# A new written-out order for a delta-rule attention with routed attention experts, and two GpSimd scalings in four pieces

## The chip, the cores and the metric

The kernel runs on one core of a Trainium2 chip. The metric is the device time of one execution in microseconds. Shown are three runs of the kernel before, and one profiled execution, from which all rows come. PE is TensorE, DVE is VectorE, ACT is ScalarE, POOL is GpSimd, SP is SyncE, which here only issues DMAs.

## The reference

The first half is linear attention with a delta rule, for 4 batches, 8 heads, 768 tokens and a head size of 48:

```python
k_n = k / (np.linalg.norm(k, axis=-1, keepdims=True) + 1e-06)
for t in range(S):
    y[:, :, t] = np.einsum('bhd,bhde->bhe', q[:, :, t], state)
    v_old = np.einsum('bhde,bhd->bhe', state, kt)
    state = state + bt[..., None] * np.einsum('bhd,bhe->bhde', kt, vt - v_old)
```

The second half takes y as x (768 tokens by 384 for each batch) and runs 4 attention experts of head size 64 over it, causal, with softmax; each token's two best experts by `x @ w_gate` are weighted by a softmax over the two and summed after the output projection `wo`.

## The kernel before

**Units and chunks.** The tokens are worked as 6 units `n` (0 to 5): units 0 to 2 are the three stretches of 256 tokens of the first pair of batches, 3 to 5 those of the second. A unit has 4 chunks `c` of 64 tokens, and a chunk has 16 heads (2 batches by 8 heads). Within a chunk the delta rule is a triangular system, so each unit needs the inverse of 32x32 triangular blocks, all 128 partitions by 32x32 at a time, and then a correction between the halves of each 64-token block.

**The inverse of a unit.** `gk` (TensorE) makes the Gram products of the keys, `ek` copies them to TN and TG. `si` transposes on VectorE into BB. `pre.n.0` to `pre.n.7` are small instructions on 32 columns: inverse square roots of the diagonal by Newton steps (`rr`, `g`, `nn`), then the scales `aa` and `na`; the last number of the token says VectorE (1) or GpSimd (2). `pa` multiplies BB (128 x 32 x 32) by `aa`, `sv.n.1` to `sv.n.30` are elimination steps (each a product into `tp` and a subtraction from `bl`, of i x (31 - i) columns), `sv.n.31` a triangular mask, `pz` a second scaling and a copy of the diagonal. Then `so` and `sn` transpose back, `sc1` copies halves, `ma` and `mb` (TensorE) join the halves, and `ea` and `eb` (8 small copies each from PSUM) follow them. Unit 0 has another way: `en` masks the Gram blocks, `sb.1` to `sb.15` eliminate 16x16 blocks on VectorE, and `zx`, `zp`, `ze` finish each chunk's inverse by block products on TensorE.

**The recurrence.** For each chunk: `gq` and `eq` make the masked query-key products `pm`, `vt` scales the values (kv by `nt`), `ks` multiplies the keys with the state SB, `ex` subtracts this from the values into XB, `uu` applies the inverse, `eu` copies, `st` and `es` update the state, `yq` and `yu` make the output, `eh` and `el` split it into a rounded part and a rest in XH, and `hx` moves rows between partitions by DMA.

**The experts.** Per unit and batch: `pj`, `ph`, `pl` are queries and keys, `pv`, `ev`, `eg` values and gate logits, `gates` the routing, `mx`, `em`, `mp`, `mr`, `er` the row maxima ahead of the softmax, `sc`, `xp`, `av`, `oa` scores, exponentials, weighted values and their copy, `nm`, `on` the normalization, `ft`, `fh`, `fl`, `fo`, `eo`, `do` the projection and the store.

**What sets the order.** Tiles are scheduled by hand: the string `ORDER` lists about 1390 tokens, each the name of a small function with its arguments, `name.args:bank`. A loop at the end of the kernel calls them one by one, and every engine issues its own instructions in that order, so the list is at once the program of five in-order queues. For functions with an engine argument, 0 is ScalarE, 1 VectorE and 2 GpSimd. The digit behind the colon is one of four PSUM buffers `ps0` to `ps3` of two banks each. `fill.n` issues n matmuls of zeros, which nothing reads. `lk`, `lh`, `lv`, `lw`, `lc` are loads on SyncE's queue (`lh` with a last 1 on ScalarE's); weights are loaded into the tiles AT, rounded by `wh` on ScalarE, and `wl` takes the rest. `eq.n.c.0` is a copy on ScalarE and a masking product on GpSimd, `eq.n.c.1` one product on VectorE straight from PSUM.

The line numbers that the rows name: L182 all matmuls, L186 and L188 copies on ScalarE and VectorE, L302 `wl`, L351 `en`, L358 `eq`, L362 `si`, L382 to L404 `pre`, L408 `pa`, L412 `pz`, L422 and L424 `sv`, L427 `zt`, L438 and L439 `sb`, L454 `sn`, L458 `so`, L473 `zx`, L531 `vt`, L540 `ex`, L704 the end of `mp`, L763 to L765 `nm`, L768 `on`.

Of the kernel before, what the change touches and what calls it, by code (L numbers as in the profile page):

```python
# [47 lines left out]
gq.0.1:1 eq.0.1.0:1 gq.0.0:2 sn.0 zx.0.0.0 zx.1.0.0 fill.15:0 zp.0.0:0 lw.6 zp.0.1:0 wh.1.0 si.1 pre.1.0.1 zx.0.1.0  # L48
wl.4.2 vt.0.2.2 wh.6.1 ze.0.1.0:0 zp.1.0:3 ze.0.0.0:0 pre.1.1.2 zx.1.1.0 zp.1.1:3 ze.1.1.1:3 wl.6.1 lk.2.0 pre.1.2.1
pre.1.3.2 zp.0.2:1 wl.1.2 wh.5.0 zp.0.3:1 ze.1.0.0:3 ze.0.3.0:1 ze.0.2.0:1 zp.1.2:0 zp.1.3:0 pre.1.4.1 pre.1.5.2  # L50
zp.0.4:3 eq.0.0.1:2 ze.1.3.0:0 ze.1.2.0:0 ze.0.4.0:3 vt.0.0.2 fill.4:1 uu.0.0:1 zx.2.0.0 eu.0.0.0:1 pa.1.1 pre.1.6.1
sv.1.1.1 sv.1.2.1 zp.1.4:2 zx.3.0.0 st.0.0:3 zp.2.0:0 ze.2.0.0:0 es.0.0:3 yu.0.0:1 fill.2:3 zp.2.1:0 sv.1.3.2 sv.1.4.2
sv.1.5.1 yq.0.1:3 eh.0.0.0:1 zx.2.1.0 ze.1.4.0:2 ze.2.1.0:0 pre.1.7.2 el.0.0:1 sv.1.6.1 sv.1.7.1 ks.0.1:1 zx.3.1.0
zp.2.2:2 ex.0.1:1 uu.0.1:0 zp.3.0:1 ze.2.2.0:2 fill.2:0 zp.2.3:2 sv.1.8.2 sv.1.9.2 ze.2.3.0:2 sv.1.10.2 sv.1.11.2
sv.1.12.1 wl.5.2 sv.1.13.2 eu.0.1.0:0 ze.3.0.0:1 yu.0.1:3 st.0.1:0 es.0.1:0 eh.0.1.1:3 zp.3.1:1 fill.5:2 zp.2.4:2
ze.2.4.0:2 el.0.1:3 lv.1.0 lv.0.3 ze.3.1.1:1 ks.0.2:0 gq.0.3:3 ex.0.2:0 lk.2.1 eq.0.3.1:3 yq.0.2:1 sv.1.14.2 sv.1.15.2
sv.1.16.1 fill.7:2 uu.0.2:2 sv.1.17.1 zp.3.2:0 sv.1.18.1 zp.3.3:0 sv.1.19.1 eu.0.2.0:2 yu.0.2:1 fill.5:3 st.0.2:3
ze.3.2.0:0 ze.3.3.0:0 lk.2.2 vt.0.3.2 vt.1.0.2 hx.0.0 es.0.2:3 zp.3.4:2 eh.0.2.1:1 sv.1.20.2 el.0.2:1 sv.1.21.2
sv.1.22.2 ks.0.3:0 sv.1.23.1 ex.0.3:0 yq.0.3:3 ze.3.4.0:2 uu.0.3:2 lv.1.1 vt.1.1.1 eu.0.3.0:2 vo gk.2.1:1 fill.2:0
yu.0.3:3 eh.0.3.1:3 sv.1.24.2 ek.2.1.0:1 sv.1.25.2 sv.1.26.2 gq.1.0:0 el.0.3:3 eq.1.0.1:0 sv.1.27.2 sv.1.28.2  # L60
sv.1.29.2 fill.8:2 st.0.3:2 sv.1.30.2 sv.1.31.2 gk.2.2:1 gk.2.0:3 ek.2.2.0:1 es.0.3:2 lk.2.3 pv.0.0:0 hx.0.1 lv.1.2
ek.2.0.1:3 ev.0.0.1:0 gk.2.3:2 ks.1.0:1 gq.1.2:3 eg.0.0:0 pj.0.0.0:0 pz.1.2 ek.2.3.0:2 eq.1.2.0:3 so.1 si.2 pre.2.0.1
sc1.1.1.0 sc1.1.0.0 pre.2.1.2 ph.0.0.0.0:0 ex.1.0:1 pl.0.0.0:0 pre.2.2.1 pj.0.0.1:2 ma.1:3 sn.1 vt.1.2.2 pre.2.3.2
pre.2.4.1 ea.1.0.1.0.1:3 gq.1.1:1 eq.1.1.0:1 pre.2.5.2 ea.1.0.1.1.1:3 pa.2.2 sv.2.1.2 sv.2.2.2 sv.2.3.2 ea.1.1.1.0.1:3
ea.1.1.0.0.0:3 pre.2.6.1 sv.2.4.2 sv.2.5.2 pv.0.1:0 ea.1.0.0.1.0:3 ph.0.0.1.0:2 pj.0.1.1:1 ea.1.1.0.1.0:3
ea.1.1.1.1.0:3 ea.1.0.0.0.0:3 ph.0.1.1.0:1 mb.1:3 eg.0.1:0 gates.0.0 sv.2.6.2 sv.2.7.2 eb.1.0.1.1.0:3 pl.0.0.1:2
sv.2.8.2 sv.2.9.2 ev.0.1.1:0 pre.2.7.1 eb.1.1.0.0.0:3 eb.1.0.0.1.0:3 eb.1.0.1.0.0:3 eb.1.1.1.0.0:3 pj.0.1.0:2
ph.0.1.0.0:2 eb.1.1.0.1.1:3 eb.1.1.1.1.1:3 yq.1.0:0 eb.1.0.0.0.1:3 pl.0.1.1:1 uu.1.0:3 mx.0.0.0.0:1 lk.3.0 pl.0.1.0:2
mx.0.0.1.0:2 eu.1.0.0:3 em.0.0.0.0:1 yu.1.0:0 mx.0.1.1.0:3 em.0.0.1.0:2 eh.1.0.0:0 st.1.0:1 lv.1.3 gq.1.3:2 el.1.0:0
mp.0.0.2 es.1.0:1 mr.0.0:0 er.0.0.0:0 mx.0.1.0.0:1 em.0.1.1.0:3 em.0.1.0.0:1 sv.2.10.2 sc.0.0.0.0:0 eq.1.3.0:2  # L70
xp.0.0.0.0:0 ks.1.1:3 gk.3.0:2 yq.1.1:1 ek.3.0.0:2 mp.0.1.1 mr.0.1:0 er.0.1.0:0 ex.1.1:3 lk.3.1 sc.0.0.1.0:3 uu.1.1:2
# [101 lines left out]
def tile_kernel(ctx, tc, kq, kv, beta, wqk, wvg, wo, consts, out):  # L173
# [232 lines left out]
    def pa(n, e):  # L406
        BL = BB[n % 2]
        (V, G)[e - 1].tensor_tensor(BL, BL, aa[n % 2][:, None, :].to_broadcast([128, 32, 32]), op=OP.mult)  # L408

    def pz(n, e):  # L410
        BL, a = BB[n % 2], aa[n % 2]
        (V, G)[e - 1].tensor_tensor(BL, BL, na[n % 2][:, :, None].to_broadcast([128, 32, 32]), op=OP.mult)  # L412
# [470 lines left out]
```

## Time and profile before

| | |
|---|---|
| median of 3 runs | 448.09 us (445.79 to 450.54) |
| the profiled execution's own time | 449.58 us |
| its span, first to last instruction | 447.9 us |
| mean granted TensorE clock | 0.937 |
| busy: TensorE, VectorE, GpSimd, ScalarE | 391.5, 301.2, 219.8, 180.8 us |
| instructions: matmuls, VectorE, GpSimd, ScalarE | 10444, 598, 381, 344 |

In the rows below, a row of the timeline has the start and the duration in us, the engine, the line, the operation, what it writes and reads, its shape and count, and in brackets the idle time of the engine before it with what ended it. A row of the grouped view has the count, the busy time in us, the mean of one in ns and the idle time ahead of the group. PE rows of several matmuls are merged.

### The profile page before, as it was taken

What the parts mean: (1) busy time and instruction counts of PE and PEld (TensorE: products, weight loads), DVE (VectorE), ACT (ScalarE), POOL (GpSimd) and SP (SyncE); (2) the same over time, 40 slices, a digit from 0 to 9 for tenths busy, and PEclk for the clock granted to TensorE, in tenths of its full rate; (3) what the DMA queues carried; (4) which work ended last, traced back from release to release, by engine and by line L of the source; (5) the groups of instructions that cost most, each with busy time, mean ns of one, the idle gap of its engine ahead of it and who ended that gap; (6) DMA issues with size and microseconds to landing.
All of it is one profiled execution on the core that took longest, in us unless ns stands there. A gap on an engine that the chain in (4) does not pass through costs nothing.

```text
span 447.9 us, 22876 instructions
## 1 busy us (share of the span) xinstructions
PE 391.5 (87%) x10444; PEld 356.2 (80%) x10444; DVE 301.2 (67%) x598; ACT 180.8 (40%) x344; POOL 219.8 (49%) x381
## 2 busy tenths in 40 slices
...
PEclk9685998999999969999869799998999999999999
...
GB/s 195 258 154 1 5 96 103 81 14 50 99 70 95 127 1 121 82 110 50 6 33 128 77 40 58 1 37 4 91 74 84 84 21 3 23 37 37 3 4 72
DMA packets 15441, 29.45 MB, mean 66 GB/s; under 512 B 2800, under 2 KB 8944, under 8 KB 15344
## 3 DMA queue, kind: packets, MB, share of 16 engines
...
q10 hardware_dynamic: 256, 0.39, 0.4%
...
## 4 chain that ended last, share of the span: by engine, by line
PE 54%; DVE 23%; POOL 11%; issue 5%; ACT 4%; DMA 2%; ACTq 0%; DVEq 0%; POOLq 0%
PE ps L182 54%; POOL bl L422 3%; POOL tp L424 3%; DVE mx L686 2%; DVE bl L362 2%; DMA kq<-in_kq_dram 2%; POOL bl L408 2%; DVE bl L439 2%; DVE xh L592 1%; DVE tn L438 1%; DVE tt L458 1%; DVE tp L424 1%; ACT tt L186 1%; POOL kv L531 1%; DVE sb L564 1%
## 5 line engine op out<-in xcount | busy, mean ns | idle before, releaser
L424 POOL TENSOR_TENSOR tp<-bl 128x84 f32<-128x84 f32 (+13 forms) x128 | 63.6, 497 | 29.8 <-DVE bl L422 19.0
L422 POOL TENSOR_TENSOR bl<-bl,tp 128x84 f32<-128x84 f32 (+13 forms) x128 | 67.7, 529 | 10.0
L745 ACT ACTIVATE at<-ps 128x768 f32<-128x768 f32 (+1 forms) x48 | 43.1, 918 | 42.2 <-PE ps L182 40.3
L686 DVE TENSOR_REDUCE mx<-ps 128x2 f32<-128x1024 f32 (+3 forms) x48 | 44.2, 950 | 9.8 <-PE ps L182 9.7
L182 PE MATMUL ps<-xh,wqkh 128*128 128x256 f32 x288 | 44.7, 292 | 0.0
L182 PE MATMUL ps<-vs,at 128*64 128x65 f32 x1344 | 43.6, 223 | 0.0
L182 PE MATMUL ps<-kq 48*64 48x64 f32 x1536 | 34.4, 229 | 9.8 <-DMA kq<-in_kq_dram 5.7
L182 PEld LDWEIGHTS ps<-vs,at 128*64 128x64 f32 x1344 | 40.8, 138 | 2.2 <-issue 0.9
L186 ACT ACTIVATE tt<-ps 32x256 f32<-32x256 f32 (+2 forms) x83 | 32.1, 386 | 22.3 <-PE ps L182 19.4
L358 POOL TENSOR_TENSOR pm<-pm,cst 128x512 f32<-128x512 f32 x14 | 18.0, 1283 | 45.1 <-ACT pm L357 45.0
L182 PEld LDWEIGHTS ps<-kq 48*64 48x64 f32 x1536 | 29.0, 141 | 13.7 <-issue 6.4
L182 PEld LDWEIGHTS ps<-xh,wqkh 128*128 128x128 f32 x288 | 38.6, 194 | 1.3 <-ACT ot L186 0.4
L182 PE MATMUL ps<-qh,kh 64*128 64x256 f32 x192 | 34.9, 354 | 0.0
L182 PEld LDWEIGHTS <-ide 64*128 64x128 bf16 (+1 forms) x516 | 26.9, 100 | 6.8 <-issue 1.9
L182 PE MATMUL ps<-ql,kh 64*128 64x256 f32 x192 | 28.1, 283 | 0.0
L182 PE MATMUL ps<-qh,kl 64*128 64x256 f32 x192 | 27.8, 280 | 0.0
L182 PE MATMUL ps<-mr,sel 64*128 64x256 bf16 x192 | 27.3, 271 | 0.0
L182 PE MATMUL ps<-mask,ide 64*128 64x128 bf16 (+1 forms) x384 | 25.6, 208 | 1.4 <-issue 1.4
L182 PE MATMUL ps<-kh,qh 64*128 64x512 f32 (+3 forms) x128 | 24.9, 415 | 1.3 <-DVE kl L621 1.0
L182 PE MATMUL ps<-xh,wqkl 128*128 128x256 f32 x144 | 25.5, 287 | 0.0
L182 PE MATMUL ps<-wvgh,xh 128*128 128x260 f32 x144 | 25.4, 300 | 0.0
L186 ACT ACTIVATE ub<-ps 128x384 f32<-128x384 f32 x20 | 9.8, 490 | 35.6 <-PE ps L182 28.2
...
## 6 DMA issues: line engine op xcount, KB each, us to landing
...
```

Source lines behind the costliest of these rows:

```text
L182: T.matmul(o, lhsT=a, rhs=b, start=start, stop=stop, skip_group_check=True)
L186: S.activation(o, x, AF.Copy, **({} if scale is None else {"scale": scale}))
L358: (V if e else G).tensor_tensor(t, P if e else t, pmask[:, None, None, :].to_broadcast([128, 2, 4, 64]), op=OP.mult)
L362: V.transpose(BB[n % 2], d.rearrange("p t j -> p j t"))
L408: (V, G)[e - 1].tensor_tensor(BL, BL, aa[n % 2][:, None, :].to_broadcast([128, 32, 32]), op=OP.mult)
L422: e.tensor_tensor(X[:, a:b, i + 1:], X[:, a:b, i + 1:], tv, op=OP.subtract)
L424: e.tensor_tensor(tv, R[:, :, i + 1:].to_broadcast([128, w, m]), X[:, a:b, i:i + 1].to_broadcast([128, w, m]), op=OP.mult)
L438: E.tensor_tensor(tv, BD[:, :, i:i + 1, i + 1:].to_broadcast([128, 2, i, m]), BD[:, :, 0:i, i:i + 1].to_broadcast([128, 2, i, m]), op=OP.mult)
L439: E.tensor_tensor(x, x, tv, op=OP.add)
L458: V.transpose(d.rearrange("p t i -> p i t"), BB[n % 2].rearrange("p l i -> p i l"))
L686: V.tensor_reduce(d, two(k)[:, :, a:a + 128 * (k1 - k0)], axis=AX.X, op=OP.max)
L745: S.activation(at_of(n, b, y, kp)[:, :, 0:w], two(k)[:, :, 0:w], AF.Exp, scale=0.125)
```

## The change

`ORDER` is replaced as a whole: nearly the same tokens (1387 for 1395) in another order, with other PSUM buffers and, for part of them, other engines. By the list, the tokens that change their engine are, in numbers (before, after):

| token | engine | before | after |
|---|---|---|---|
| eq | VectorE alone / ScalarE and GpSimd | 10 / 14 | 17 / 7 |
| oa | VectorE / ScalarE | 12 / 12 | 3 / 21 |
| ea | VectorE / ScalarE | 17 / 23 | 14 / 26 |
| eb | VectorE / ScalarE | 15 / 25 | 11 / 29 |
| eh | VectorE / ScalarE | 8 / 16 | 5 / 19 |
| ph | VectorE / ScalarE | 5 / 19 | 7 / 17 |
| ev | VectorE / ScalarE | 4 / 8 | 2 / 10 |
| mp | VectorE / GpSimd | 6 / 6 | 3 / 9 |
| sv | VectorE / GpSimd | 22 / 133 | 27 / 128 |
| pa | VectorE / GpSimd | 1 / 4 | 0 / 5 |
| pz | VectorE / GpSimd | 1 / 4 | 1 / 4 |
| vt | VectorE / GpSimd | 7 / 17 | 6 / 18 |
| fill | matmuls | 132 in 18 places | 126 in 10 places |

One or two tokens each of `en`, `zx`, `ek`, `ze`, `eu`, `er`, `on`, `fh`, `sc1` and `wh` change too. The second part of the change: where `pa` or `pz` runs on GpSimd (e = 2), it is four instructions of 8 x 32 columns in place of one of 32 x 32; on VectorE (e = 1) it stays one.

The start and the end of the list, and a stretch around the join of unit 2, after the change:

```diff
+lz lc.0 zg init lh.0.2.0.0 lh.0.3.0.1 fill.22:0 gk.0.2:0 lh.0.1.0.1 lh.0.0.0.0 lc.1 lw.5 en.2.1:0 ed.2:0 gk.0.3:1
+gk.0.1:2 gk.0.0:3 ed.3:1 ed.1:2 ed.0:3 lw.3 en.3.0:1 si.0 pre.0.0.1 lw.0 pre.0.1.1 lh.0.3.1.0 pre.0.2.1 en.1.0:2
+wh.3.0 wh.5.0 pre.0.3.1 lh.0.2.1.0 pre.0.4.1 pre.0.6.1 pre.0.5.1 lk.1.3 wh.0.0 wl.0.2 lk.1.0 fill.36:0 gk.1.0:0
+gk.1.3:1 zt pre.0.7.1 sb.1.1 sb.2.1 lc.2 lk.1.2 lk.1.1 lh.0.0.1.0 en.0.0:3 sb.3.1 sb.4.1 sb.5.1 sb.6.1 sb.7.1 sb.8.1
+sb.9.1 sb.10.1 sb.11.1 sb.12.1 sb.13.1 sb.14.1 sb.15.1 fill.17:2 gq.0.0:2 lv.0.2 ek.1.0.0:0 cb wl.3.2 zm ek.1.3.0:1
+gk.1.1:3 lw.4 so.0 gk.1.2:0 sn.0 ek.1.1.0:3 lw.6 wh.6.0 ek.1.2.0:0 wh.4.0 lv.0.0 gq.0.2:1 vt.0.0.2 lw.1 lh.0.1.1.0
+wl.4.2 eq.0.0.0:2 zx.0.0.0 gq.0.1:3 lv.0.1 si.1 pre.1.0.1 eq.0.1.0:3 zx.1.0.0 pre.1.1.1 zx.0.1.0 fill.6:0 zp.0.0:0
...
+pre.3.1.2 eq.2.2.0:2 fo.0.1.1:1 pre.3.2.1 ma.2:3 eo.0.1.0:1 sn.2 ea.2.0.0.0.1:3 do.0.1 pre.3.3.2 ks.2.0:0
+ea.2.0.1.1.0:3 vt.2.2.2 ea.2.1.1.1.0:3 ea.2.1.1.0.0:3 ea.2.0.0.1.0:3 ea.2.1.0.0.0:3 pre.3.4.1 ea.2.0.1.0.0:3
+ea.2.1.0.1.0:3 ex.2.0:0 pre.3.5.2 pv.1.1:1 pj.1.1.1:2 ph.1.1.1.0:2 ev.1.1.0:1 eg.1.1:1 pre.3.7.2 mx.1.0.1.0:0
+gates.1.1 mx.1.0.0.0:1 em.1.0.1.0:0 mb.2:3 pl.1.1.1:2 em.1.0.0.0:1 pj.1.1.0:0 yq.2.0:2 eb.2.1.1.1.0:3 eb.2.0.0.1.0:3
...
+fo.5.0.1:0 eo.5.0.0:0 do.5.0 av.5.1.1.2:2 oa.5.1.1.0:2 nm.5.1 on.5.1.1 fill.18:1 ft.5.1:1 fh.5.1.0:1 fl.5.1:1
+fill.14:3 fo.5.1.0:3 fo.5.1.1:3 eo.5.1.0:3 do.5.1
...
     def pa(n, e):
-        BL = BB[n % 2]
-        (V, G)[e - 1].tensor_tensor(BL, BL, aa[n % 2][:, None, :].to_broadcast([128, 32, 32]), op=OP.mult)
+        for q in range(e * e):
+            BL = BB[n % 2][:, 32 // (e * e) * q:32 // (e * e) * (q + 1)]
+            (V, G)[e - 1].tensor_tensor(BL, BL, aa[n % 2][:, None, :].to_broadcast([128, 32 // (e * e), 32]), op=OP.mult)
 
     def pz(n, e):
         BL, a = BB[n % 2], aa[n % 2]
-        (V, G)[e - 1].tensor_tensor(BL, BL, na[n % 2][:, :, None].to_broadcast([128, 32, 32]), op=OP.mult)
+        for q in range(e * e):
+            w = slice(32 // (e * e) * q, 32 // (e * e) * (q + 1))
+            (V, G)[e - 1].tensor_tensor(BL[:, w], BL[:, w], na[n % 2][:, w, None].to_broadcast([128, 32 // (e * e), 32]), op=OP.mult)
         (V, G)[e - 1].tensor_copy(BL.rearrange("p j i -> p (j i)")[:, 0:1024:33], a)
```

The same stretches of the list before:

```diff
-lz lc.0 lh.0.3.0.1 fill.22:0 gk.0.3:0 lh.0.1.0.1 lh.0.2.0.0 ed.3:0 fill.1:1 gk.0.1:1 ed.1:1 gk.0.2:2 ed.2:2 lh.0.0.0.0
-gk.0.0:3 ed.0:3 si.0 init lk.1.2 pre.0.0.1 pre.0.1.1 pre.0.2.1 lc.2 lh.0.3.1.0 pre.0.3.1 pre.0.4.1 lw.2 en.1.0:1
-en.2.0:2 zm lh.0.0.1.0 lh.0.2.1.0 pre.0.6.1 lk.1.0 lc.1 pre.0.5.1 en.3.0:0 zt pre.0.7.1 gk.1.2:1 ek.1.2.0:1 cb sb.1.1
-sb.2.1 sb.3.1 gk.1.0:2 lw.0 wh.2.0 lw.3 gq.0.2:1 sb.4.1 sb.5.1 en.0.0:3 eq.0.2.0:1 sb.6.1 lv.0.1 sb.7.1 lh.0.1.1.0
-lk.1.1 sb.8.1 zg wh.3.0 lk.1.3 fill.28:0 gk.1.1:0 wh.0.0 sb.9.1 sb.10.1 sb.11.1 sb.12.1 sb.13.1 sb.14.1 sb.15.1 wl.0.2
-wl.2.2 lw.4 lv.0.2 lw.5 wl.3.2 so.0 fill.5:3 gk.1.3:3 lw.1 lv.0.0 ek.1.0.0:2 ek.1.1.0:0 vt.0.1.2 wh.4.0 ek.1.3.0:3
...
-ea.2.1.1.0.0:0 lk.4.0 pre.3.3.2 ea.2.0.0.0.0:0 pre.3.4.1 ea.2.1.1.1.1:0
-pre.3.5.2 pre.3.7.1 ea.2.0.0.1.1:0 ea.2.0.1.0.0:0 ea.2.0.1.1.1:0 eg.1.1:2 do.0.1 gates.1.1 vt.2.2.2
-ea.2.1.0.0.0:0 ea.2.1.0.1.0:0 ev.1.1.0:2 ph.1.1.1.0:3 mb.2:0 eb.2.0.1.0.0:0 eb.2.0.0.1.0:0 eb.2.1.0.0.1:0
...
-do.5.0 on.5.1.1 fill.8:0 ft.5.1:0 fh.5.1.0:0 fl.5.1:0 fill.8:1 fo.5.1.0:1 fo.5.1.1:1 eo.5.1.0:1 do.5.1
```

More of the change, by code (lines that the diff above doesn't have):

```diff
@@ L47 @@
-wl.2.2 lw.4 lv.0.2 lw.5 wl.3.2 so.0 fill.5:3 gk.1.3:3 lw.1 lv.0.0 ek.1.0.0:2 ek.1.1.0:0 vt.0.1.2 wh.4.0 ek.1.3.0:3
[L48 to L71, printed above, removed]
```

209 lines of the change are left out of this document (114 added, 95 removed).

## The prediction

> **What bounds the kernel now.** I read the page first: span, engines, granted clock, chain. Then the busy time by stage, the first 50 us engine by engine, the waits of TensorE, and the grouped rows of what the change touches. From the page:
>
> ```profile
> span 447.9 us, 22876 instructions
> ...
> PE 391.5 (87%) x10444; PEld 356.2 (80%) x10444; DVE 301.2 (67%) x598; ACT 180.8 (40%) x344; POOL 219.8 (49%) x381
> ...
> PEclk9685998999999969999869799998999999999999
> ...
> PE 54%; DVE 23%; POOL 11%; issue 5%; ACT 4%; DMA 2%; ACTq 0%; DVEq 0%; POOLq 0%
> ```
>
> TensorE is busy for 87% and has 54% of the chain; the other half of the chain is VectorE and GpSimd, so what can be won is where TensorE waits. The stages (columns: stretch, its length, busy time and instructions of PE, PEld, DVE, ACT, POOL, granted clock, DMA share, GB/s):
>
> ```profile
> 0.00:37.75 37.75, 18.40 (x424) 15.90 (x424) 28.66 (x57) 15.66 (x38) 17.97 (x22) 0.76 0.69 180
> 37.75:349.70 311.95, 281.22 (x8001) 257.12 (x8002) 221.79 (x432) 131.88 (x258) 196.92 (x352) 0.94 0.22 63
> 349.70:443.60 93.90, 91.90 (x2020) 83.16 (x2020) 50.79 (x111) 32.48 (x48) 4.87 (x7) 1.00 0.10 28
> 159.60:166.40 6.80, 6.57 (x102) 6.26 (x106) 3.62 (x10) 3.09 (x8) 5.86 (x13) 0.50 0.01 2
> 214.20:217.60 3.40, 3.40 (x16) 3.40 (x17) 2.63 (x3) 0.00 (x0) 2.77 (x9) 0.50 0.00 0
> 224.40:231.20 6.80, 6.64 (x112) 5.58 (x116) 3.76 (x11) 2.42 (x7) 6.04 (x10) 0.50 0.00 0
> ```
>
> The start, up to the first product of the block inverse at 37.75, leaves TensorE idle for 37.75 - 18.40 = 19.4 us. The middle, up to the first state product of the last unit at 349.70, leaves it idle for 311.95 - 281.22 = 30.7 us, and in places at half clock: the last three rows are three such stretches, 6.8, 3.4 and 6.8 us at 0.50. The end is full (91.90 of 93.90) at full clock: there a new order can win next to nothing.
>
> **The start, part by part.** The path is VectorE's: transpose, inverse square root, 15 elimination steps of unit 0, transpose, then one ScalarE copy, then TensorE. VectorE first, then GpSimd, then TensorE:
>
> ```profile
> 11.91 0.92 DVE L382 TENSOR_SCALAR g<-bl 128x32 int32<-128x32 int32 x1
> ...
> 24.98 1.24 DVE L439 TENSOR_TENSOR bl<-bl,tn 128x100 f32<-128x100 f32 x1
> ...
> 29.08 0.78 DVE L439 TENSOR_TENSOR bl<-bl,tn 128x112 f32<-128x112 f32 x1
> ...
> 31.41 0.26 DVE L439 TENSOR_TENSOR bl<-bl,tn 128x100 f32<-128x100 f32 x1
> ...
> 33.79 0.69 DVE L441 TENSOR_TENSOR bl<-bl,aa 128x512 f32<-128x512 f32 x1
> 34.75 1.91 DVE L458 STREAM_TRANSPOSE vs<-bl 128x1024 f32<-128x1024 f32 x1
> ```
>
> ```profile
> 24.79 1.31 POOL L302 TENSOR_TENSOR wvgl<-at,wvgh 128x512 fp32r<-128x512 f32 x1
> ...
> 28.88 0.85 POOL L531 TENSOR_TENSOR kv<-kv,nt 128x384 f32<-128x384 f32 x1
> ```
>
> ```profile
> 37.75 1.97 PE L182 MATMUL ps<-tt,vs 64*64 64x64 f32 x32 [11.32 <-ACT vs L473]
> ```
>
> The same product of 100 columns takes 1.24 us while GpSimd works (24.79 to 26.10) and 0.26 us once GpSimd has stopped (its last one ends at 29.73). From 11.91 (0.92 us) to 29.08 (0.78 us) there are 12 such drawn-out VectorE instructions, 13.0 us in all; eleven of them at about 0.2 to 0.27 and one of 512 columns at 0.69 would be 3.1. So some 9.9 us of this path are VectorE standing behind 12 GpSimd instructions, about 0.8 us for each.
>
> In the new order GpSimd has fewer of them in that stretch. One of the three masks of the units' diagonal blocks that it made goes to VectorE (en.2); the pm product of chunk 2 goes to VectorE and those of chunks 0 and 1 move behind the elimination in the queue; wl.2 moves behind it; the memset zg goes to the front. Left beside the path are en.1's end, wl.0, zt, en.0 and wl.3, five; two or three more (vt.0.0, wl.4, the pm product of chunk 0) come as soon as their loads land, perhaps after the path has ended. Five to eight at 0.8 us are 4.0 to 6.4 us, so the path wins 9.9 less that: 3.5 to 5.9. I take 5.
>
> Against it stand two moves. ScalarE now runs `init` (a table load and a small activation) ahead of its two loads lh.0.3 and lh.0.1, so these leave later; the path needs all four chunks, of which two are SyncE's, and the queue is no shorter than before: 0 to 1.5 us, I take 0.5. And en.2 (0.69 us, by the 512-column row) stands on VectorE ahead of three of the four `ed`, which wait for their loads anyway: nothing, 0.7 if the loads are early. lw.4 and the loads behind it on SyncE now wait for `cb`, and the last that TensorE needs ahead of the inverse, lh.0.1.1, has 5.4 MB ahead of or in it: at the 180 KB per us of the first row it lands at about 30 us, when the first product would come at 33 anyway; a lower rate costs what it is late by, 1 to 2 us. The start: -4.5, bounds -6 and +1.
>
> **The middle.** VectorE, then GpSimd, then TensorE, at three of its places:
>
> ```profile
> 155.28 2.37 DVE L404 TENSOR_SCALAR na<-aa 128x32 f32<-128x32 f32 x1
> ...
> 209.35 0.20 DVE L764 RECIPROCAL rsm<-rsm 128x8 f32<-128x8 f32 x1
> 209.59 1.99 DVE L765 TENSOR_TENSOR rsm<-gt,rsm 128x8 f32<-128x8 f32 x1
> ...
> 212.22 0.17 DVE L404 TENSOR_SCALAR na<-aa 128x32 f32<-128x32 f32 x1
> ```
>
> ```profile
> 155.25 2.36 POOL L408 TENSOR_TENSOR bl<-bl,aa 128x1024 f32<-128x1024 f32 x1
> ...
> 209.17 2.39 POOL L408 TENSOR_TENSOR bl<-bl,aa 128x1024 f32<-128x1024 f32 x1
> ```
>
> ```profile
> 159.83 1.99 PE L182 MATMUL ps<-bl,tn 32*64 32x64 f32 x64 [3.54 <-POOL bl L422]
> ...
> 212.36 0.69 PE L182 MATMUL ps<-cst,on 64*64 64x64 f32 x32 [1.30 <-DVE on L768]
> ...
> 224.56 1.72 PE L182 MATMUL ps<-bl,tn 32*64 32x64 f32 x53 [2.27 <-ACT bl L186]
> ```
>
> A VectorE instruction of 32 columns (0.17 us at 212.22) takes 2.37 us beside the row scaling `pa` of unit 3 on GpSimd, and ends with it; behind it in VectorE's queue stand copies `ea` that mb.2 needs, and TensorE waits 3.54 us. At 209.17 the same scaling of unit 4 holds the normalization product (1.99 us), and ft.1.1 waits 1.30. Not all of VectorE is held: the reciprocal at 209.35 took 0.20 beside the same scaling.
>
> The price of these places with the clock that follows: mb.2 3.54 plus half of 6.57 = 6.8 us; ft.1.1 1.30 plus half of 3.40 = 3.0; mb.3 2.27 plus half of 6.64 = 5.6; together 15.4. Each step of it in the new order: `pa` and `pz` on GpSimd come in four pieces of 256 columns, so a held VectorE instruction waits for one piece; pre.3.7 leaves VectorE; of the eight `ea` of units 2 and 3 one each is left on VectorE (three each now); and ahead of mb.2 TensorE has ks, pv, pj and two mx. But TensorE's order is new everywhere, with waits of its own that this trace cannot show. I count half of the 15.4 as won and nothing for the other waits of the middle: -8, bounds -18 (these and a few more go) and +10 (as many come anew as go).
>
> The TensorE page of the Trainium skill (TensorE: Matmul & The Clock Gate, What's actually happening) has the clock halved after at least one idle window of about 3.4 us. Here the half clock of 214.2 came after a wait of 1.30, so the measurement decides; by the page only the wait of mb.2 would carry a clock loss, and half of the three places would be 5.2 rather than 7.7 us.
>
> What the moves cost:
>
> ```profile
> L358 POOL TENSOR_TENSOR pm<-pm,cst 128x512 f32<-128x512 f32 x14 | 18.0, 1283 | 45.1 <-ACT pm L357 45.0
> ...
> L182 PE MATMUL ps<-ide 128*128 128x192 bf16 x132 | 16.5, 276 | 1.1 <-DVE ide L194 1.1
> ...
> L408 POOL TENSOR_TENSOR bl<-bl,aa 128x1024 f32<-128x1024 f32 x4 | 9.5, 2372 | 4.8 <-DVE aa L398 4.7
> ...
> L412 POOL TENSOR_TENSOR bl<-bl,na 128x1024 f32<-128x1024 f32 x4 | 7.7, 1914 | 0.3
> ...
> L358 DVE TENSOR_TENSOR pm<-ps,cst 128x512 f32<-128x512 f32 x10 | 6.8, 677 | 1.5 <-PE ps L182 1.5
> ```
>
> ```profile
> L424 POOL TENSOR_TENSOR tp<-bl 128x240 f32<-128x240 f32 x8 | 5.7, 712 | 2.4 <-DVE bl L422 2.0
> ```
>
> ```profile
> L182 PE MATMUL ps<-tt,tn 32*64 32x64 f32 x320 | 5.8, 220 | 0.0
> ```
>
> Net, seven of the 14 pm products go from ScalarE and GpSimd to VectorE alone: GpSimd loses 7 x 1.28 = 9.0 us and VectorE gains 7 x 0.68 = 4.7, which at 67% busy it has room for. A piece of a scaling is priced by the nearest row, 240 columns at 0.71: four are 2.8 to 3.0 us for 2.37 or 1.91. Without a fixed cost four are just 2.37 or 1.91; at 0.76 a piece they are 0.7 to 1.1 more. I take 0.5 for each of nine scalings on GpSimd (five `pa`, four `pz`). It lies in the chain of the next unit's inverse, whose first product, ma, never kept TensorE waiting (0.0 idle before 320 matmuls): nothing, 4.5 us if that cover were gone.
>
> Fillers go from 132 to 126 matmuls, at most 6 x 0.28 = 1.7 us less; the last 32 now stand ahead of ft and fo of the last block, in place of 16, where VectorE and ScalarE are waited for: +0.5.
>
> **The sum.** -4.5 - 8 + 0.5 = -12, against the profiled execution's 449.58 (span 447.9): 437.6. The median of the runs, 448.09, is 1.5 below that execution, so on the median: 436, rounded up to 437.
>
> **The rivals.** (1) Only the start is won, and the middle trades its waits: 448.1 - 4.5 + 0.5 = 444. For it: the middle's 30.7 us of waits have many causes, ScalarE's queue at mb.3 among them. (2) The pieces do not open the way, because GpSimd has its next piece ready when one ends. Against it: in the start single VectorE instructions came through between GpSimd's, each after about one. For it: no row shows four pieces in a row. Then ft.1.1's and part of mb.2's price stay, 441. (3) TensorE's work alone sets the time and the orders are as good as each other: 448. Against it: 50 us of waits. (4) Slower: elimination steps handed back and forth. A step on VectorE waits for GpSimd's step before it, with all of VectorE's queue behind it:
>
> ```profile
> 128.04 0.39 DVE L424 TENSOR_TENSOR tp<-bl 128x220 f32<-128x220 f32 x1 [3.44 <-POOL bl L422]
> ```
>
> ```profile
> 130.19 0.68 PE L182 MATMUL ps<-xb,tt 64*64 64x48 f32 x32 [2.03 <-DVE xb L540]
> ```
>
> Here VectorE stood for 3.44 us, and uu.1.2 for 2.03 behind the XB that was queued there. By the lists of steps VectorE takes over from GpSimd ten times in units 1 to 5 before (4, 3, 1, 0, 2) and twelve after (5, 0, 1, 2, 4). One costs some 2.0 plus a half-clock stretch of 3.4 at half, 3.7 us. Beyond three more than now the start's gain is gone; with six, 448.1 - 4.5 + 22 less the middle's 8 is 458.
>
> **How the numbers follow.** Forecast (both terms, 437) 0.58; (1) 0.17; (2) 0.08; (3) 0.07; (4) 0.10. A measurement of this kernel tells about 1% from no change, so faster is below 443.6 and slower above 452.6. Faster: 0.58, a third of (1) and most of (2): 0.69. Same: the rest of (1) and (2), and (3): 0.21. Slower: (4), 0.10. The forecast's own range is 428 to 443, by the bounds of start and middle; taking in (1), (2) and (3) it is 427 to 449, which leaves out (4) and the forecast's best end.
>
> **What would show it.** In the new profile the first product of the inverse (tt by vs) starts at about 33 instead of 37.75, and the elimination steps of unit 0 have at most eight drawn-out instructions. GpSimd's scalings show pieces of 0.5 to 0.8 us, and no small VectorE instruction beside them is longer than about 0.8. TensorE's idle time between that first product and the last unit's first state product is below 25 us, with fewer stretches at half clock. I am wrong if the first product is not earlier, if the middle's idle time is 30 us or more, or if waits on XB or `bl` of over 2 us turn up behind elimination steps on VectorE.

## The result, and the profile after

After the change the median of four runs is 431.77 us (428.74 to 433.45), against 448.0 us for the kernel before beside it: a ratio of 0.963, with a 95% interval of 0.955 to 0.971. (The ratios here leave disturbed runs out and the medians don't, so a ratio can differ a little from the quotient of two medians.) That is a gain of 16.2 us where 11 had been forecast (437, range 427 to 449). The profiled execution of the changed kernel took 430.98 us. From its page (the numbers of lines of code shift by a few from kernel to kernel with the length of the list: L442 here is L439 of the kernel before):

```profile
span 429.0 us, 22899 instructions
PE 383.8 (89%) x10438; PEld 350.0 (82%) x10438; DVE 293.5 (68%) x585; ACT 184.4 (43%) x357; POOL 213.7 (50%) x402
PEclk9865999698999999999999999999999999999998
PE 55%; DVE 22%; POOL 11%; issue 5%; ACT 4%; DMA 2%; SPq 1%; DVEq 0%; ACTq 0%; POOLq 0%
```

The span is 18.9 us shorter than that of the profiled execution before, which was itself one of the longer ones (the medians are 16.2 apart), and TensorE's busy time only 7.7 us (391.5 to 383.8): the other 11.2 us are waits. The clock digits show where part of the busy time went. Before, the half clock came back in six places between the start and the end; now two are left, the 6 in the eighth slice and the 8 in the tenth. The chain of waits looks as before: its shares alone don't tell a better order from a worse one.

The stages, cut at the same events as before: the first product of the block inverse (34.97) and the first `uu` of the last unit (326.90, where before had 349.70):

```profile
0.00:34.97 34.97, 20.64 (x434) 18.25 (x434) 25.43 (x58) 15.01 (x37) 13.22 (x18) 0.79 0.69 194
34.97:326.90 291.93, 268.67 (x7936) 246.29 (x7938) 215.51 (x421) 136.18 (x271) 195.79 (x370) 0.97 0.24 68
326.90:426.00 99.10, 94.51 (x2085) 85.45 (x2073) 52.55 (x108) 33.23 (x50) 4.69 (x14) 1.00 0.09 25
```

TensorE's idle time in the middle fell from 30.7 to 291.93 - 268.67 = 23.3 us, in the start from 19.4 to 14.3.

**The start.** First VectorE in the timeline, then GpSimd, then TensorE:

```profile
24.84 0.89 DVE L442 TENSOR_TENSOR bl<-bl,tn 128x112 f32<-128x112 f32 x1
...
26.07 0.81 DVE L442 TENSOR_TENSOR bl<-bl,tn 128x108 f32<-128x108 f32 x1
26.91 1.22 DVE L441 TENSOR_TENSOR tn<-bl 128x100 f32<-128x100 f32 x1
28.17 0.26 DVE L442 TENSOR_TENSOR bl<-bl,tn 128x100 f32<-128x100 f32 x1
...
31.97 1.91 DVE L461 STREAM_TRANSPOSE vs<-bl 128x1024 f32<-128x1024 f32 x1 [0.51 <-DVE bl L445]
```

```profile
24.77 0.83 POOL L534 TENSOR_TENSOR kv<-kv,nt 128x384 f32<-128x384 f32 x1 [4.47 <-DMA kv<-in_kv_dram]
26.01 0.75 POOL L302 TENSOR_TENSOR wvgl<-at,wvgh 128x268 fp32r<-128x268 f32 x1 [0.41 <-ACT wvgh L186]
26.71 1.30 POOL L358 TENSOR_TENSOR pm<-pm,cst 128x512 f32<-128x512 f32 x1
```

```profile
34.97 1.97 PE L182 MATMUL ps<-tt,vs 64*64 64x64 f32 x32 [5.46 <-ACT vs L476]
```

Three GpSimd products, three drawn-out VectorE instructions, each ending 0.12 or 0.13 us behind one of them: vt.0.0, wl.4 and the mask product of chunk 0, whose data had landed before the path was over. Seven drawn-out instructions are left of twelve. The first product stands at 34.97 instead of 37.75.

**The middle, unit by unit.** Each row reaches from the first `uu` of a unit to that of the next, the last one to the end. Before, then after:

```profile
49.80:106.60 56.80, 47.73 (x1519) 43.71 (x1520) 40.35 (x76) 22.41 (x50) 37.98 (x71) 0.97 0.21 59
106.60:165.90 59.30, 52.71 (x1489) 48.03 (x1489) 46.15 (x92) 27.40 (x57) 41.67 (x74) 0.95 0.30 83
165.90:230.40 64.50, 59.69 (x1563) 53.67 (x1562) 49.55 (x89) 27.59 (x53) 47.53 (x86) 0.92 0.23 64
230.40:304.80 74.40, 67.57 (x1887) 62.02 (x1890) 49.19 (x103) 30.43 (x53) 46.80 (x85) 0.94 0.20 57
304.80:349.70 44.90, 41.83 (x1272) 38.27 (x1265) 28.41 (x59) 18.34 (x33) 18.95 (x30) 0.98 0.22 65
349.70:447.90 98.20, 91.92 (x2020) 83.16 (x2020) 50.79 (x111) 33.29 (x49) 4.87 (x7) 0.99 0.10 31
```

```profile
47.00:102.60 55.60, 46.55 (x1494) 43.64 (x1498) 38.34 (x75) 24.59 (x54) 36.21 (x67) 0.91 0.21 60
102.60:159.60 57.00, 50.31 (x1508) 45.59 (x1496) 42.58 (x82) 26.05 (x56) 45.77 (x87) 1.00 0.29 80
159.60:219.40 59.80, 56.32 (x1550) 50.44 (x1550) 48.06 (x86) 28.39 (x56) 43.78 (x88) 1.00 0.28 76
219.40:285.90 66.50, 63.38 (x1853) 57.85 (x1851) 45.99 (x94) 32.60 (x61) 43.99 (x90) 1.00 0.22 63
285.90:326.90 41.00, 40.37 (x1268) 37.30 (x1266) 31.26 (x66) 18.01 (x34) 17.34 (x28) 1.00 0.25 76
326.90:429.00 102.10, 94.51 (x2085) 85.45 (x2073) 52.55 (x108) 33.23 (x50) 4.69 (x14) 0.99 0.10 28
```

This table is the account of the change. The first row starts 2.8 us earlier. The five rows of the middle are 1.2, 2.3, 4.7, 7.9 and 3.9 us shorter, 20.0 together. The end is 3.9 longer: 2.6 of it is busy time, with 65 more matmuls (17 more fillers and 32 query-key products among them), and 1.3 is idle time. 2.8 + 20.0 - 3.9 = 18.9. The sum of the five rows is firmer than the single row: the same list with whole scalings (experiment 2, with the same time) has 51.8, 59.1, 62.4, 63.5 and 42.4, which differ from the rows here by up to 3.8 us and add up to 279.2 against 279.9.

At the three places that the prediction priced, the waits are gone: mb.2 (154.19), ft.1.1 (204.78) and mb.3 (215.60) start without one.

```profile
154.19 1.16 PE L182 MATMUL ps<-bl,tn 32*64 32x64 f32 x64
...
204.78 0.65 PE L182 MATMUL ps<-cst,on 64*64 64x64 f32 x32
...
215.60 1.16 PE L182 MATMUL ps<-bl,tn 32*64 32x64 f32 x64
```

New waits came in between: 1.40 us ahead of ma.2, 1.23 at 153.72 and 1.78 at 213.26. TensorE's longest one behind the start is now 1.78 us, where it was 3.54.

What the 20.0 are made of can be read from the same rows. TensorE's idle time is 30.4 us before and 23.0 after (length less busy time, summed over the five rows): 7.4. Its busy time falls by 12.6. How much of that is the clock, the stretches at half clock show: the sum over the six of before (70.80 to 74.20, 159.60 to 166.40, 214.20 to 217.60, 224.40 to 231.20, 244.90 to 251.70, 302.90 to 306.30), and the two of after:

```profile
sum 30.60, PE 29.11 PEld 27.14 DVE 16.15 ACT 8.85 POOL 24.79; mean PE 4.85 PEld 4.52 DVE 2.69 ACT 1.48 POOL 4.13
```

```profile
75.10:81.90 6.80, 5.69 (x172) 5.39 (x162) 2.77 (x7) 3.80 (x10) 4.98 (x11) 0.50 0.47 137
99.00:102.40 3.40, 3.40 (x35) 3.17 (x37) 1.89 (x7) 2.22 (x6) 2.90 (x7) 0.51 0.00 0
```

29.1 us of work at half clock before cost 14.6, and 9.1 after cost 4.5: 10.0 of the 12.6. The other 2.6 us go with 57 fewer matmuls.

This is busy time, and not yet the kernel's. For 42 executions of the kernel before, of 443 to 451 us, the granted clock is on record; the span times what the clock lacks to 1 lies between 18.8 and 32.3 us. The third of them that lost least (22.1 on average) took 446.8 us, and the third that lost most (28.3) took 447.5: 6.2 us more lost to the clock went with only 0.7 us more time. In the ten executions of experiment 10 a straight line through such pairs gives 0.7 us for each us lost. So how much of the 20.0 us the slower clock caused is not shown.

**The moved and split instructions**, in the grouped view after:

```profile
L409 POOL TENSOR_TENSOR bl<-bl,aa 128x256 f32<-128x256 f32 x20 | 14.0, 735 | 2.6 <-DVE aa L398 2.5
L415 POOL TENSOR_TENSOR bl<-bl,na 128x256 f32<-128x256 f32 x16 | 9.9, 648 | 0.3
L358 POOL TENSOR_TENSOR pm<-pm,cst 128x512 f32<-128x512 f32 x7 | 9.2, 1315 | 14.7 <-ACT pm L357 14.7
L358 DVE TENSOR_TENSOR pm<-ps,cst 128x512 f32<-128x512 f32 x17 | 11.6, 685 | 3.8 <-PE ps L182 3.8
```

Five scalings `pa` in 20 pieces take 14.0 us, 2.80 each, against 2.37 whole. Seven mask products have gone from GpSimd to VectorE at 0.685 us.

### The profile page after: what moved, and what is told of

Same layout as the page of the kernel before. It is cut to its first block, busy times and chain, and to the rows that moved or that the text cites. A ratio compares the mean times of both kernels' runs of the same rounds, so it can differ in the third digit from the quotient of the medians.

```text
span 429.0 us, 22899 instructions
## 1 busy us (share of the span) xinstructions
PE 383.8 (89%) x10438; PEld 350.0 (82%) x10438; DVE 293.5 (68%) x585; ACT 184.4 (43%) x357; POOL 213.7 (50%) x402
## 4 chain that ended last, share of the span: by engine, by line
PE 55%; DVE 22%; POOL 11%; issue 5%; ACT 4%; DMA 2%; SPq 1%; DVEq 0%; ACTq 0%; POOLq 0%
PE ps L182 55%; POOL bl L425 4%; POOL tp L427 4%; DVE mx L689 3%; DVE tn L457 2%; ACT bl L186 2%; DVE bl L362 2%; DVE tp L427 1%; DVE bl L442 1%; DVE tt L461 1%; DVE tn L441 1%; DVE bl L425 1%; SPq L601 1%; DVE bl L188 1%; DMA xh<-xh 1%
## 5 line engine op out<-in xcount | busy, mean ns | idle before, releaser
L427 POOL TENSOR_TENSOR tp<-bl 128x84 f32<-128x84 f32 (+14 forms) x123 | 61.2, 498 | 29.1 <-DVE bl L425 13.6
L425 POOL TENSOR_TENSOR bl<-bl,tp 128x84 f32<-128x84 f32 (+14 forms) x123 | 64.1, 521 | 9.6
L182 PE MATMUL ps<-kq 48*64 48x64 f32 x1536 | 35.7, 236 | 10.0 <-DMA kq<-in_kq_dram 7.7
L186 ACT ACTIVATE tt<-ps 32x256 f32<-32x256 f32 (+2 forms) x90 | 34.7, 386 | 19.7 <-PE ps L182 13.2
L182 PEld LDWEIGHTS ps<-kq 48*64 48x64 f32 x1536 | 31.2, 148 | 12.8 <-DMA kq<-in_kq_dram 5.2
L182 PE MATMUL ps<-qh,kh 64*128 64x256 f32 x192 | 33.9, 348 | 0.3 <-DVE gd L650 0.3
L534 POOL TENSOR_TENSOR kv<-kv,nt 128x384 f32<-128x384 f32 x18 | 15.1, 841 | 25.3 <-DMA kv<-in_kv_dram 17.3
L182 PE MATMUL ps<-mr,sel 64*128 64x256 bf16 x192 | 26.2, 267 | 0.0
L182 PE MATMUL ps<-kh,qh 64*128 64x512 f32 (+3 forms) x128 | 23.7, 399 | 1.6 <-DVE lg L640 1.2
L182 PE MATMUL ps<-wvgh,xh 128*128 128x260 f32 x144 | 24.2, 290 | 0.0
L186 ACT ACTIVATE ub<-ps 128x384 f32<-128x384 f32 x21 | 10.3, 491 | 26.7 <-PE ps L182 26.1
```

The lines of the kernel that those rows point to most:

```text
L182: T.matmul(o, lhsT=a, rhs=b, start=start, stop=stop, skip_group_check=True)
L186: S.activation(o, x, AF.Copy, **({} if scale is None else {"scale": scale}))
L425: e.tensor_tensor(X[:, a:b, i + 1:], X[:, a:b, i + 1:], tv, op=OP.subtract)
L427: e.tensor_tensor(tv, R[:, :, i + 1:].to_broadcast([128, w, m]), X[:, a:b, i:i + 1].to_broadcast([128, w, m]), op=OP.mult)
L534: (V, G)[e - 1].tensor_tensor(v, v, nt[n % 2][:, c * NP:c * NP + NP, None].to_broadcast([128, NP, HD]), op=OP.mult)
```

## The experiments

The theory from the prediction: VectorE stands behind GpSimd, the pieces and the moved products shorten that, and the new order takes away waits that the clock makes dearer. The rivals: the list alone does it, without the pieces; or only the order, or only the choice of engines; or the clock alone. In the diffs below `+` and `-` stand for tokens of the list. In the numbers, the kernel before is that of the same comparison (446.9, 447.0 and 447.5 us). First a table of what the profiles show: the start of the first inverse product, of the first `uu` of units 0 to 5, and the end, in us; the last column is the sum, to about 0.1 us, of the stretches at half clock that begin between 45 and 420 us.

```
                 inverse  uu.0  uu.1   uu.2   uu.3   uu.4   uu.5    end  half clock
before              37.8  49.8 106.6  165.9  230.4  304.8  349.7  447.9  30.6
after               35.0  47.0 102.6  159.6  219.4  285.9  326.9  429.0  10.2
pieces only         38.1  50.1 106.8  164.1  224.5  299.0  344.4  442.6  20.4
list only           35.5  46.3  98.1  157.2  219.5  283.0  325.4  427.1  10.2
new start only      35.4  46.9 103.6  160.0  222.1  296.6  342.6  440.5  30.6
old start           38.4  49.2 106.3  165.4  225.1  291.3  332.7  434.5  17.0
order, old engines  33.9  53.1 108.8  181.3  245.4  317.5  366.4  470.7  37.5
six moved           33.2  47.1 103.6  161.3  224.2  297.8  342.8  440.9  17.0
more fillers        37.5  48.2 103.8  164.2  232.3  305.1  349.4  447.5  17.0
nine eq back        34.5  45.7 100.8  162.6  222.2  290.1  332.9  435.0  13.6
copies back         35.4  47.0 100.2  160.0  224.4  295.0  341.9  445.1  17.0
VectorE/GpSimd back 35.4  51.2 109.1  180.3  241.9  310.4  353.6  455.1  40.9
further moved       34.2  44.1 100.5  160.6  223.1  288.1  329.6  431.3  23.8
```

**1. The pieces only**: the list of before, with the scalings in four pieces.

```diff
     def pa(n, e):
-        BL = BB[n % 2]
...
+        for q in range(e * e):
...
```

> The list of before, with pa and pz on GpSimd in four pieces. Theory 'pieces': the small VectorE instructions that stood 2.37 and 1.99 us beside a whole scaling stand at most 0.8, mb.2 waits about 1.9 us instead of 3.5 and ft.1.1 not at all, and the half clock behind them goes: 448 falls to 440-445. Rival 'the list': the pieces shorten the two held instructions but the waits of TensorE come from the order of its work, so 446-449.

Measured: 446.05 us, ratio 0.997 (0.993 to 1.002). VectorE, then TensorE, in its timeline:

```profile
156.22 0.76 DVE L402 TENSOR_SCALAR na<-aa 128x32 f32<-128x32 f32 x1
```

```profile
159.17 1.41 PE L180 MATMUL ps<-bl,tn 32*64 32x64 f32 x64 [1.93 <-ACT bl L184]
...
219.82 1.16 PE L180 MATMUL ps<-bl,tn 32*64 32x64 f32 x64 [2.46 <-ACT bl L184]
```

The instruction that had stood for 2.37 us is through in 0.76: it gets in after one piece, and the rival by which GpSimd's next piece is always ready falls. ft.1.1 waits 0.17 us instead of 1.30, as the first theory had it, and 20.4 us are at half clock in place of 30.6. But mb.2 still waits 1.93 us, now for ScalarE, and mb.3 2.46. A wait that several engines cause at once is not gone with the first of them, and the time does not change beyond the interval, which allows for a gain of 0.7% or 3 us.

**2. The list only**: the list of after, with whole scalings.

```diff
     def pa(n, e):
-        for q in range(e * e):
...
+        BL = BB[n % 2]
...
```

> The list of after, with each scaling as one instruction. Theory 'pieces': small VectorE instructions stand up to 2.4 us beside the scalings again, TensorE waits at two or three joins and the clock drops there: 436-441 for 431.8. Rival 'the list': 431-434.

Measured: 431.03 us, 0.963 (0.954 to 0.972). The whole gain is in the list; the pieces add nothing that shows within these 0.9%. mb.2, ft.1.1 and mb.3 have no wait here either, so in the new list it is not the pieces that took those waits away.

**3. and 4. Order and engines, each alone.** In the list of after, the 171 tokens whose engine the change had changed get their old one; and the other way round, in the list of before they get the new one. The scalings are in four pieces in both.

```diff
-sv.2.24.2
+sv.2.24.1
...
-oa.1.1.1.0:0
+oa.1.1.1.1:0
-ea.3.1.0.1.0:2
+ea.3.1.0.1.1:2
```

> The order and the PSUM buffers of after, with every token on the engine that it has in the list of before (171 tokens), scalings on GpSimd in pieces. Theory 'order': the order of TensorE's work carries the gain, 432-437. Rival 'engines': the moves (eq off GpSimd, oa and ea off VectorE) carry it, 440-448.

> The order and the PSUM buffers of before, with every token on the engine that it has in the list of after (171 tokens), scalings on GpSimd in pieces. Theory 'order': 443-450, since the engines were chosen for another order. Rival 'engines': 434-441.

Measured: the order with the old engines 469.48 us, 1.050 (1.043 to 1.057); the old order with the new engines 474.26 us, 1.051 (1.040 to 1.062). No theory had that. Each half of the change alone makes the kernel 5% slower, and both together make it 4% faster. TensorE's longest wait with the old engines:

```profile
134.26 1.14 PE L179 MATMUL ps<-cst,on 64*64 64x64 f32 x32 [9.08 <-DVE on L768]
```

It is in ft.0.0, for which TensorE does not wait at all before and waits 0.34 us after. What causes it is told with experiment 11.

**5. and 6. The start, and the rest.** The new list up to zp.0.0 and the old one from there; and the reverse. Tokens that stand on the other side of the cut in the other list are put ahead of or behind it.

```diff
-lz lc.0 lh.0.3.0.1 fill.22:0 gk.0.3:0 lh.0.1.0.1
+lz lc.0 zg init lh.0.2.0.0 lh.0.3.0.1 fill.22:0 gk.0.2:0 lh.0.1.0.1
...
 zp.0.0:0 
```

> The list of after up to the first product of the block inverse (zp.0.0), without gq.0.2, then what is left of the list of before in its own order. Theory 'the start adds up': the 2.8 us by which that product comes earlier are kept to the end, 444-446 for 448. Rival 'the start is given back': the later joins wait for other things, 447-450. Second rival, 'the start counts double': unit 1's scaling came 7.5 us earlier in the whole change, 440-443.

> The reverse: the list of before up to zp.0.0, without gq.0.0, then what is left of the list of after. Theory 'the start adds up': 434-436 for 431.8. Rival 'given back': 431-433. Rival 'counts double': 437-441.

Measured: the new start on the old list 443.38 us, 0.988 (0.981 to 0.994); the old start on the new list 436.98 us, 0.976 (0.971 to 0.981). By the ratios the start is worth 1.25% or 5.6 us in the one, and 1.3% or 5.9 us in the other (0.976 less 0.963); the rest of the list is worth 2.4% or 10.7 to 11.0 us. The medians give 3.6 and 5.2 for the start, and the interval of the first comparison alone reaches from 2.7 to 8.5. Within that the two parts add up to the whole: what the start wins is not lost in a later wait.

**7. The shared access in the start.** In the list of before, six GpSimd products are moved out of the elimination of unit 0, behind the first products of the block inverse; nothing else is changed. One of them, wl.0, reads its tile there after the load lw.6 has written over it, so the rest part of the first query and key weights is not that of the reference in this kernel; the instructions and their sizes are the same.

```diff
-wl.0.2 wl.2.2
...
-wl.3.2
...
-vt.0.1.2
...
-wl.4.2 vt.0.2.2
...
+wl.0.2 wl.2.2 wl.3.2 vt.0.1.2 wl.4.2 vt.0.2.2
```

> The list of before, with six GpSimd products (wl.0, wl.2, wl.3, wl.4, vt.0.1, vt.0.2) taken out of the stretch of unit 0's elimination and put behind pre.1.1. Theory 'shared access': each of them had drawn out a VectorE instruction by about 0.8 us, so the first product of the inverse comes at 32.5-34 instead of 37.75, and VectorE's steps there take 0.19-0.27 us each. Rival 'the loads': the drawn-out steps only filled time that loads or copies set anyway, 36.5-38. The whole: 443-446 or 447-450.

Measured over ten runs: 446.19 us, 0.993 (0.989 to 0.998). VectorE, GpSimd and TensorE in its timeline:

```profile
20.51 0.19 DVE L436 TENSOR_TENSOR tn<-bl 128x28 f32<-128x28 f32 x1
...
26.19 1.19 DVE L436 TENSOR_TENSOR tn<-bl 128x88 f32<-128x88 f32 x1
27.41 0.25 DVE L437 TENSOR_TENSOR bl<-bl,tn 128x88 f32<-128x88 f32 x1
...
28.73 0.20 DVE L436 TENSOR_TENSOR tn<-bl 128x28 f32<-128x28 f32 x1
```

```profile
19.69 1.93 POOL L309 MEMSET tt<- 32x1024 f32 x2
25.89 1.38 POOL L356 TENSOR_TENSOR pm<-pm,cst 128x512 f32<-128x512 f32 x1 [4.28 <-ACT pm L355]
...
46.27 0.82 POOL L529 TENSOR_TENSOR kv<-kv,nt 128x384 f32<-128x384 f32 x1
```

```profile
33.16 1.97 PE L180 MATMUL ps<-tt,vs 64*64 64x64 f32 x32 [7.41 <-ACT vs L471]
...
47.14 1.11 PE L180 MATMUL ps<-kv,tt 64*64 64x48 f32 x32 [3.29 <-POOL kv L529]
```

Without GpSimd beside it every step takes 0.19 to 0.28 us, and the one GpSimd product left (25.89) draws out one step to 1.19. The first product comes at 33.16, 4.6 us earlier: that VectorE stands behind GpSimd is shown to cost the start these 4.6 us. But uu.0.0 needs vt.0.0 from GpSimd, which now stands in that queue behind the six moved products and ends at 47.09; TensorE waits 3.29 us for it. So 2.7 of the 4.6 are kept at uu.0.0, and 0.7% or 3.1 us at the end.

**8. The clock.** In the list of before, 108 more filler matmuls at six of the waits of the middle.

```diff
+fill.20:2
...
+fill.28:2
...
+fill.18:1
```

> The list of before with 108 fillers more, put into six of TensorE's waits (after uu.0.2, ahead of mb.2, mb.3, ft.1.1, mr.3.0 and yq.3.2), so that TensorE is not idle there. Theory 'clock': the half-clock stretches behind these waits go (30 us of them, worth 15) while the waits stay, 434-441. Rival 'slack': what runs at half clock has room, or the fillers delay what follows, 445-450.

Measured: 454.75 us, 1.010 (1.003 to 1.018), slower by 1%. Its profiled execution (449.27, its fastest run) has 17.0 us at half clock in place of 30.6 and is no shorter for it. At mb.3:

```profile
224.03 2.50 PE L180 MATMUL ps<-ide 128*128 128x192 bf16 x18 [2.20 <-DVE ql L619]
226.45 1.99 PE L180 MATMUL ps<-bl,tn 32*64 32x64 f32 x64
```

The fillers themselves first wait 2.20 us, until VectorE has read what stood in their bank (ql), and then hold mb.3 back, at half clock. So this doesn't tell what the clock alone is worth: the fillers cost as much as they save.

**9. to 11. Which engines matter.** In the list of after, three parts of the 171 tokens get their old engine: the nine `eq`, the 96 copies out of PSUM between ScalarE and VectorE, and the 66 others, nearly all between VectorE and GpSimd.

```diff
-eq.3.0.1:3
+eq.3.0.0:3
```

> The whole of after, with only the nine pm products eq whose engine changed put back (eight to ScalarE and GpSimd, one to VectorE). Theory 'shared access in the middle': eight GpSimd products of 1.3 us more draw out VectorE's small instructions and the elimination steps, 434-438 for 431.8. Theory 'no single group, order and engines fit each other': 433-440, any change of engines in a fixed list costs. Rival 'eq does not matter': 430-433.

```diff
-ea.2.0.1.1.0:3
+ea.2.0.1.1.1:3
...
-oa.1.0.1.0:0
+oa.1.0.1.1:0
```

> The whole of after, with the 96 copies out of PSUM whose engine changed (oa, ea, eb, eh, eu, ph, ev, er, fh, ek, ze) put back between ScalarE and VectorE. Theory 'fit': most of the 38 us of the kernel with all engines put back, 450-465. Theory 'shared access in the middle': these do not use GpSimd, so little, 433-438.

```diff
-sv.2.24.2
+sv.2.24.1
-sv.2.25.2
+sv.2.25.1
-sv.2.26.2
+sv.2.26.1
```

> The whole of after, with the 66 tokens put back that changed between VectorE and GpSimd or stand in their chains (sv, pre, pa, pz, vt, mp, on, zx, en, sc1, wh). Theory 'fit': 440-455, a step that waits for the other engine's step stops the queue behind it. Theory 'shared access in the middle': 440-450 too, with drawn-out VectorE instructions up from 22 us to over 27; without that rise it is waiting in the queue and not shared access.

Measured: nine `eq` back 436.25 us, 0.977 (0.972 to 0.982); copies back 451.29, 1.008 (1.004 to 1.012); VectorE and GpSimd back 455.74, 1.019 (1.014 to 1.024). Less the 0.963 of after that is 1.4, 4.5 and 5.6%, or 6.2, 20.3 and 25.2 us. All 171 together cost 8.7%, 38.9 us: less than the sum of the parts, as with waits that stand behind each other. For the last of them, VectorE, GpSimd and TensorE:

```profile
131.54 0.39 DVE L424 TENSOR_TENSOR tp<-bl 128x220 f32<-128x220 f32 x1 [7.22 <-POOL bl L422]
...
133.09 0.68 DVE L768 TENSOR_TENSOR on<-os,rsm 128x512 f32<-128x512 f32 x1
```

```profile
124.47 0.61 POOL L424 TENSOR_TENSOR tp<-bl 128x240 f32<-128x240 f32 x1 [4.52 <-DVE bl L422]
...
130.83 0.68 POOL L422 TENSOR_TENSOR bl<-bl,tp 128x228 f32<-128x228 f32 x1
```

```profile
133.83 1.14 PE L179 MATMUL ps<-cst,on 64*64 64x64 f32 x32 [9.10 <-DVE on L768]
```

This is the longest wait of experiment 3 again. sv.2.14, sv.2.20, sv.2.21 and sv.2.24 to sv.2.26 stand on VectorE, and in the new order on.0.0 is queued behind sv.2.21. sv.2.20 has to wait until GpSimd has done the steps before it, which GpSimd had itself begun 4.52 us late, behind sv.2.14 on VectorE. The normalization's weights are ready at 123.57, ahead of sv.2.14 in the queue, but on.0.0 starts at 133.09; ft.0.0 waits 9.10 us, and TensorE is at half clock from 129.1 to 142.7. The stretch from uu.1.0 to uu.2.0, in which this lies, is 14.2 us longer than in after, of 26.1 for the whole profile. In the list of after these steps are GpSimd's, and VectorE passes on to on.0.0. The shared access does not explain it: VectorE's drawn-out time (what its instructions took over the shortest of the same line, tiles and form, after 45 us) is 21.7 us here and 22.0 in after.

With the copies put back no single wait stands out: TensorE's longest behind the start is 2.15 us, and what is lost is spread over all stretches from uu.1.0 to uu.5.0. VectorE is busy for 302.3 us there and ScalarE for 174.1, where after has 293.5 and 184.4, so more work on VectorE is not excluded as the cause.

**12. A version that might beat both.** In the list of after, three more GpSimd instructions leave the elimination of unit 0 (vt.0.0 and wl.4 go behind it, eq.0.0 to VectorE), and 20 fillers in place of 6 stand ahead of the first inverse product.

```diff
-vt.0.0.2
...
-wl.4.2 eq.0.0.0:2
+eq.0.0.1:2
+vt.0.0.2 wl.4.2
-fill.6:0
+fill.20:0
```

> After, with the start changed further: vt.0.0 and wl.4 behind eq.0.1 in GpSimd's queue and eq.0.0 on VectorE behind the last transposition, so that three GpSimd products leave the elimination, and 20 fillers instead of 6 ahead of the first product. Theory 'shared access in the start': the first product at 32.5-33.5 instead of 35.0, the whole 428-430. Theory 'clock' adds up to 2 us if the product's 5.9 us at half clock go. Rival 'given back at vt.0.0 or the loads': 431-433.

Measured: 433.10 us, 0.969 (0.965 to 0.973), not faster than after. The first product came at 34.22 and not at 32.5 to 33.5, and here the new fillers are what holds it: ScalarE's copy for it ends at 31.99, but the 20 fillers run from 30.90 to 34.28. uu.0.0 starts at 44.1, 2.9 us earlier than in after, and by uu.3.0 it is 3.7 us late; 23.8 us are at half clock in place of 10.2. The list behind the start is the same; what may move the clock's stretches about is told in the last section, but it was not shown to be the cause here.

## Why the prediction came out as it did

**The start: the mechanism right, the size off.** "VectorE standing behind GpSimd" is shown by experiment 7, and the price of about 0.8 us for each GpSimd instruction by the three pairs after, which cost 0.62, 0.54 and 0.96 us over the length without GpSimd. The term was -4.5 at the first product, and -2.8 was measured, for three reasons that the rows show. Seven drawn-out instructions stayed (the forecast had five to eight, and 5 us won of the 9.9 for that; at seven 9.9 less 5.6 would have been 4.3; the twelve add up to 13.2 us and not 13.0, which changes little). The transpose si.0 starts at 10.59 instead of 9.89, 0.7 where 0.5 was taken for the later loads. And so.0 waited 0.51 us on VectorE. That the loads are the cause of the 0.7 is not shown: full clock is first granted at 10.21 in this execution and at 5.96 before, and the key products of the last two chunks take 1.2 us each where they took 0.7. Over all profiles si.0 starts between 9.7 and 10.6 with the old start and between 9.7 and 11.6 with the new one. The first product was to come at about 33 and came at 34.97. What the start is worth at the end, 3.6 to 5.9 us by experiments 5 and 6, holds the 4.5.

**The middle: direction right, size too small, and one of its steps wrong.** The three places priced at 15.4 us lie before uu.3.0, and half of it was counted as won. Between uu.1.0 and uu.3.0 the profile shows 2.3 + 4.7 = 7.0, and that of experiment 2 only 2.3: all three waits went, where half was counted, but new ones came, and whether the 7.7 were right is not settled by that. The step that failed is "nothing for the other waits of the middle": 11.8 us came between uu.3.0 and uu.5.0, and 13.4 in the profile of experiment 2. Two stretches at half clock lay there (244.9 and 302.9, 9.2 us of work, 4.6 us of loss), and idle time fell from 9.9 to 3.7 us. In all, the profile has -20.0 for the middle and +3.9 for the end, where -8 and +0.5 stood. The signs named for it came true: idle time below 25 us (23.3), two stretches at half clock for six, and no wait of TensorE on XB of over 2 us. Over more runs, by experiments 5 and 6, all behind the start is worth 10.7 to 11.0, against 7.5 forecast, and less than the 16.1 of the two profiles. That the total is nearer to the forecast than the middle is luck in part: the end's error of 3.4 us stands against the middle's.

**The range.** It was said to follow from the bounds of start and middle, but -6, -18 and +0.5 added up give 425, and +1, +10 and +0.5 give 460. What was written down, 428 to 443, is narrower; 431.77 lies in both.

**The pieces: the price right, the gain wrong.** Half a microsecond for each scaling, hidden, was right (2.80 for 2.37, and ma still hardly waits: once, 1.40 us, for a copy). But the pieces were given a share in what the waits would lose, and experiments 1 and 2 find none beyond their intervals: 0.997 (0.993 to 1.002) with the pieces alone, and 0.963 for the list with them and without.

**What the moves between engines do** was taken for a matter of load, VectorE with room at 67% and GpSimd with less to do. Experiment 11, and the longest wait of experiment 3, show that it is a matter of place in the queue as well. In experiment 11 VectorE is busy for 286.8 us and GpSimd for 213.7, where after has 293.5 and 213.7: no more work, and 25 us more. For the copies of experiment 10 and for experiment 4 the cause was not traced to a wait.

**The rivals.** (1) Only the start: fell, the old start with the rest of the new list still has 0.976. (2) The pieces don't open the way: fell for the instruction that gets in (0.76 us), but the list wins as much without the pieces. (3) TensorE's work alone sets the time: fell, idle time went and the time with it. (4) The hand-overs: it did not happen here. In the view of the waits VectorE's hand-overs are, after:

```profile
DVE tp L427 <- POOL bl L425: 8.3, 7, 2.2
```

That is 8.3 us in seven waits, the longest 2.2; before it was 8.4 in seven, the longest 3.4. But it is just what makes experiments 3 and 11 slow, and its price of 3.7 us was too low: 9.10 us and a stretch at half clock for one. Counting hand-overs (ten before, twelve after) could not tell the two lists apart; what stands behind the waiting step could.

**What stays open.** Which single wait carries how much of the middle's gain was not separated. That half clock makes up 10.0 of the 12.6 us of busy time is worked out from two profiled executions; what it costs the kernel is not shown, neither by experiment 8 nor by the 42 executions of the kernel before. In experiment 1 ten us less of it changed nothing. What took away the waits at mb.2, ft.1.1 and mb.3, the order or the engines of the copies, was not separated either.
